# A transformer block on one core: weights loaded behind x, two banks for early V tiles, and a different order of the first head groups

## The chip, the cores and the metric

The kernel runs on one core of a Trainium2 chip. A core has a matrix engine (TensorE, PE in the profile; its weight loads are listed as PEld), a vector engine (VectorE, DVE), a scalar engine (ScalarE, ACT), a general engine (GpSimd, POOL) and a queue engine (SyncE, SP). Each runs its own instructions in order and waits for the others by semaphores. Matrix products are written to PSUM, which has eight banks of 128 partitions by 512 fp32 columns; everything else lies in SBUF. DMAs are issued by an engine's queue, here SP's and, for a few, ACT's.

The metric is the time of one execution on the device, in microseconds. Lower is better.

## The reference

One transformer block with pre-norm, on 2048 rows of 512 features in bf16, with 32 heads of 16:

```python
h  = x + attention(layernorm(x))         # qkv = ln(x) @ wqkv; softmax(q k^T / 4) v; @ wo
h2 = h + glu(layernorm(h))               # (sigmoid(n @ w_gate) * (n @ w_up)) @ w_down, F = 1792
```

Heads are small, so the scores cost little arithmetic in the sums over 16 features; but 32 x 2048 x 2048 exponentials, 134 million, must be taken.

## The kernel before, in words

**Tiling.** Queries are taken in chunks c: three of 512 rows and two of 256. Heads are taken in groups g of four, eight groups in all. For each (c, g), keys are taken in blocks of 128. A *unit* (c, g, k, j) is one head's scores of one block of keys against the query chunk, a 128 x 512 tile, one PSUM bank. Three units make a *step* (`groups`, 683 of them). The main loop runs over the steps, in the order in which `units` lists them.

**A step.** `emit_scores(i)` issues the step's score matmuls (L848) into one of two PSUM tiles of three banks, pss0 and pss1, by turns. ScalarE then takes exp of the 128 x 1536 tile in one instruction (L859). In every fourth step, from step 8 on, one of the three units is taken by VectorE instead, in five instructions (L878 to L891: `exp_bits` and three more), so ScalarE's instruction is 128 x 1024; in `twice` steps a second such unit goes to VectorE in the same four steps. `emit_pv` issues the matmuls of exp with V (L929) some steps later, into the bank `acc`. Each head has V with a column of ones (`Vaug`), which gives the sum for the softmax.

Scores are kept from overflow by a bound per query: the norm of the query times the largest norm of a key, which enters the scores as one more row (`bnd`, `nks`). Query rows of the current head group are spread by DMA over the partitions of `QB` (two buffers, by turns; `emit_q_rows`, `emit_q_bound`), keys over those of `KT` (`k_spread`), both on SP's queue. The odd rows of `KT` hold ones, the unused rows of `QB` zeros; GpSimd's memsets put them there. The first two steps read a QB buffer that has no bound row yet and add the bound by a matmul of their own (L835, L838).

**Pairs.** When `pairs` is true, two heads' score matmuls, of 64 rows each, run side by side in the two halves of the array. It is true in the first 44 steps (`FIRST`), then in odd steps and around `twice` steps, except where the filler is idle.

**Fillers.** All other matrix work is a generator, `filler()`, which yields one matmul at a time: V tiles 3 to 15, then K block 1 and the Q of query chunk 0 for the same heads, blocks 2 and 3 likewise, then Q of query chunks 1 to 3, then each chunk's output projection and feed-forward (`ffn_tasks`). A block is 128 features, eight heads, two head groups. `emit_fill(i)` lets so many matmuls through at each step as `rate(i)` says; `RATES` has the rates by step modulo 4, those of the first 44 steps stand in `rate`. Steps with PV work get fewer. A `("gap", n)` holds the filler back n steps, an `("at", n)` to a step modulo 4, a `("from", n)` to step n. Fillers of this part share one PSUM bank (`ps_misc`), so a tile's matmuls wait until the tile before has been evicted.

**Prologue.** Ahead of the steps, `prologue` loads x, takes the row statistics in eight pairs of 128 rows (`stats` on VectorE, `stats_act` on ScalarE for pair 1, the inverse root on GpSimd), normalises them (`apply`, L317), transposes them on TensorE (`trans`, L324) and copies them to `xnT` on ScalarE (L326). As rows become ready it computes K block 0 in four chunks of 512 (`k_chunk`, `k_half`), Q of chunk 0 for the first eight heads (`q_chunk`), V tiles 0 to 2 (`v_tile`), the key norms, and the bound. It takes its PSUM tiles from a pool of six banks, which is closed before pss0 and pss1 are made of the same banks. The three parts of wqkv are loaded from ScalarE's queue, K's first, beside x on SP's queue.

**The order of the work** is that of the text: each engine runs its instructions in the order in which this program emits them. No scheduler reorders them.

Of the kernel before, what the change touches and what calls it, by code (L numbers as in the profile page):

```python
# [19 lines left out]
def kernel(  # L20
# [28 lines left out]
    RATES = ((2.0, 2.0, 0.0, 3.0), (2.0, 2.5, 0.0, 3.0))  # L49
    FIRST = 44  # L50
    GM = 188
# [19 lines left out]
    def pm_tile():  # L71
        return pmh["pool"].tile([P, 512], FP32, name="pm")
# [154 lines left out]
    qgs = [(c, g) for c in range(NC) for g in range(NG)]  # L227
# [20 lines left out]
    NV0 = 3  # L248
# [4 lines left out]

    def prologue(pro):
# [3 lines left out]
        for part in (1, 0, 2):  # L258
            nc.scalar.dma_start(out=wqkv_sb[:, :, part * D:(part + 1) * D],
                                in_=wqkv_v[:, :, part * D:(part + 1) * D])  # L260
# [3 lines left out]
        nc.gpsimd.memset(QB[1][:].rearrange("p j q -> p (j q)").bitcast(FP32), 0.0)  # L264
# [122 lines left out]
        fill_ones(nc.gpsimd, KT[:, 1, :])  # L387
        stats_act(1)
        nc.gpsimd.memset(QB[0][:].rearrange("p j q -> p (j q)").bitcast(FP32), 0.0)
        nc.gpsimd.memset(bnd[:].bitcast(FP32), 0.0)  # L390
        stats(2)
        nc.gpsimd.memset(Vaug[:, :, :, DH:DH + 1], 1.0)
        apply(0)
        trans(0)
        stats(3)
        apply(1)
        trans(1)
        apply(2)
# [8 lines left out]
        apply(4)  # L407
        k_chunk(1)
        norm_mm_to(acc[:], sqs["q"])
        trans(4)  # L410
        stats(6)
        apply(5)
        v_tile(0)
        norm_part_of(1)
        v_tile(1)
        trans(5)
        stats(7)
        apply(6)
        ps2 = k_mm(2)
        square(2, ps2[:])  # L420
        trans(6)
# [3 lines left out]
        k_max(pnp[0:96, :], km4 := small.tile([P, 1], FP32, name="km4"))  # L425
# [7 lines left out]
        k_copy(2, ps2)  # L433
        k_copy(3, ps3)
# [3 lines left out]
        k_fold(kd, 96, 0)  # L438
        pn3 = ps_misc.tile([P, 512], FP32, name="pm")
# [24 lines left out]
    def first_step(c):  # L464
        return NS * CHUNKS[c][0] / S if c < NC else NS
# [67 lines left out]
    def fill_q(qc):  # L533
# [19 lines left out]
        for b in range(4):  # L553
            ready.add(("b", qc, b))
# [519 lines left out]
```

## Time and profile before

| what | us |
|---|---|
| median of 3 runs | 963.19 |
| the runs | 962.74, 963.19, 966.67 |
| the profiled execution | 966.62 |
| its span, first to last instruction | 964.8 |
| ACT busy | 898.4 (93%) |
| PE busy | 832.2 (86%) |
| DVE busy | 784.4 (81%) |
| POOL busy | 36.0 (4%) |
| first exp of the steps starts at | 35.38 |
| last exp ends at | 934.80 |
| an exp of 128 x 1536 / 128 x 1024 on ACT | 1.473 to 1.486 / 1.058 to 1.068 |

Exps that follow each other without a wait overlap a little, so a row of them takes less than the sum of their lengths. A matmul's end is modelled, so a busy PE isn't PE at its peak. A window of the profile gives, for a stretch of time, the busy time and number of instructions of each engine, the granted share of TensorE's clock, and what the DMA engines moved. Step n starts where the n-th exp activation (L859) starts.

### The profile page before, as it was taken

The numbers are of one execution on the slowest core, as the hardware profiler recorded it, in microseconds if no ns is written. First come the engines' busy times: TensorE is split into PE (matmuls) and PEld (weight loads), VectorE is DVE, ScalarE is ACT, GpSimd is POOL, SyncE is SP. The second block draws the span as 40 slices with busy tenths as digits, with TensorE's granted clock in tenths as the row PEclk, the third lists the DMA queues.
The fourth block names the chain that finished last, engine by engine and source line by source line (L and its number), as shares of the span: only waits on it lengthen the run. The fifth ranks groups of instructions, "written<-read, shape, count | busy, mean of one in ns | idle before, by whom it ended". The sixth has DMA issues, their size and how long they took to land.

```text
span 964.8 us, 17172 instructions
## 1 busy us (share of the span) xinstructions
PE 832.2 (86%) x6335; PEld 338.8 (35%) x6433; DVE 784.4 (81%) x1413; ACT 898.4 (93%) x774; POOL 36.0 (4%) x55
## 2 busy tenths in 40 slices
PE   4888888888888999998788999888788999998998
PEld 2322222222222232222222233222255555555656
DVE  8389998888878888899888888898899788777653
ACT  5789999999999999999999999999998999999872
POOL 5102000000001000000000000000000000000000
PEclk9999999999999999999999999999999999999999
DMA  5102341000013000001011000000011000010010
GB/s 159 24 1 56 113 104 29 16 15 3 15 26 102 15 15 16 9 19 27 15 26 27 16 16 14 4 26 26 16 26 26 16 10 16 27 32 16 9 35 12
DMA packets 37645, 28.45 MB, mean 29 GB/s; under 512 B 17788, under 2 KB 32920, under 8 KB 37560
## 3 DMA queue, kind: packets, MB, share of 16 engines
q1 hardware_dynamic: 35832, 25.64, 10.1%
q10 hardware_dynamic: 1728, 1.70, 0.5%
q8 instruction: 50, 0.82, 0.4%
q14 instruction: 35, 0.29, 0.1%
HBM read 20.31 MB, written 2.61 MB: 24 GB/s over the span
## 4 chain that ended last, share of the span: by engine, by line
PE 43%; DVE 24%; ACT 23%; issue 6%; DMA 2%; SPq 1%; ACTq 0%; DVEq 0%
PE pss L848 20%; ACT pt L859 13%; PE acc L929 8%; PE pm L587 6%; ACT stg L859 4%; ACT wd L859 3%; DVE stg L878 3%; ACT QTu L859 2%; PE pm L603 2%; PE pm L168 2%; DVE reg L881 2%; DVE pt L891 2%; PE pm L163 2%; DVE y L887 2%; PE pm L563 1%
## 5 line engine op out<-in xcount | busy, mean ns | idle before, releaser
L848 PE MATMUL pss<-QB,KT 64*128 64x512 bf16 (+3 forms) x2533 | 475.8, 337 | 81.6 <-ACT pt L859 39.9
L859 ACT ACTIVATE pt<-pss 128x1536 bf16<-128x1536 f32 (+1 forms) x392 | 502.1, 1360 | 17.2 <-PE pss L848 11.5
L848 PEld LDWEIGHTS <-KT 64*128 64x128 bf16 (+1 forms) x2554 | 180.4, 95 | 340.3 <-issue 227.8
L859 ACT ACTIVATE stg<-pss 128x1536 bf16<-128x1536 f32 (+1 forms) x140 | 183.0, 1355 | 4.5 <-PE pss L848 3.8
L878 DVE TENSOR_SCALAR stg<-pss 128x512 int32<-128x512 f32 x123 | 84.8, 689 | 71.6 <-PE pss L848 58.1
L929 PE MATMUL acc<-pt,Vaug 128*17 128x512 bf16 (+1 forms) x1471 | 112.9, 339 | 4.6 <-DVE xs_all L903 3.4
L859 ACT ACTIVATE wd<-pss 128x1536 bf16<-128x1536 f32 (+1 forms) x80 | 103.7, 1387 | 2.5 <-PE pss L848 2.5
L859 ACT ACTIVATE QTu<-pss 128x1024 bf16<-128x1024 f32 (+1 forms) x71 | 95.6, 1346 | 1.7 <-PE pss L848 1.2
L884 DVE SCALAR_TENSOR_TENSOR y<-reg 128x512 f32<-128x512 f32 x123 | 85.2, 692 | 4.2
L887 DVE SCALAR_TENSOR_TENSOR y<-y,reg 128x512 f32<-128x512 f32 x123 | 84.2, 684 | 1.1
L929 PEld LDWEIGHTS <-Vaug 128*17 128x17 bf16 x2560 | 50.5, 89 | 97.5 <-issue 83.0
L587 PE MATMUL pm<-reg,reg 128*128 128x512 bf16 (+1 forms) x252 | 55.6, 333 | 8.8 <-DVE reg L600 6.7
L587 PE MATMUL pm<-reg,wu 128*128 128x512 bf16 (+1 forms) x280 | 58.1, 338 | 1.5 <-ACT sg L592 1.2
L603 PE MATMUL pm<-wd,reg 128*128 128x512 bf16 x173 | 51.2, 381 | 4.9 <-issue 2.9
L881 DVE TENSOR_SCALAR reg<-stg 128x512 int32<-128x512 int32 x123 | 52.0, 423 | 2.0
L929 PE MATMUL acc<-stg,Vaug 128*17 128x256 bf16 (+1 forms) x564 | 51.1, 329 | 0.7 <-DVE stg L891 0.4
L600 DVE SCALAR_TENSOR_TENSOR reg<-sg,pm 128x512 bf16<-128x512 f32 x56 | 38.2, 683 | 14.0 <-PE pm L587 13.5
L891 DVE SCALAR_TENSOR_TENSOR pt<-y,stg 128x512 bf16<-128x512 f32 x70 | 47.7, 682 | 1.8
L592 ACT ACTIVATE sg<-pm 128x512 f32<-128x512 f32 x56 | 35.6, 635 | 10.2 <-PE pm L587 9.9
L878 DVE TENSOR_SCALAR wd<-pss 128x512 int32<-128x512 f32 x45 | 30.9, 688 | 16.8 <-PE pss L848 16.0
L168 PE MATMUL pm<-reg 128*128 128x512 bf16 x114 | 37.0, 403 | 5.7 <-ACT reg L326 3.3
L149 POOL TENSOR_TENSOR rs<-ve,pw_neg 128x1 f32<-128x1 f32 x16 | 11.3, 704 | 813.5 <-DVE ve L147 813.5
(141 smaller groups left out, 712.7 us busy)
## 6 DMA issues: line engine op xcount, KB each, us to landing
rb_all<-rd SPq DMA_DIRECT2D x96, 64.0 KB
xr<-in_A_x_dram SPq DMA_DIRECT2D x16, 128.0 KB
out_dram<-ob SPq DMA_DIRECT2D x15, 128.0 KB
rb_all<-rd SPq DMA_DIRECT2D x60, 32.0 KB
reg<-in_A_x_dram SPq DMA_DIRECT2D x7, 256.0 KB
KT<-stg SPq DMA_DIRECT2D x7, 256.0 KB
reg<-in_B_w_gate_dram SPq DMA_DIRECT2D x4, 448.0 KB
wu<-in_B_w_up_dram SPq DMA_DIRECT2D x4, 448.0 KB
```

Source lines behind the costliest of these rows:

```text
L168: nc.tensor.matmul(ps[:], lhsT=wqkv_sb[:, c, w0:w0 + P], rhs=xnT[:, c, n * QC:(n + 1) * QC], start=(c == 0), stop=(c == DC - 1))
L587: nc.tensor.matmul(ps[:, i * w:(i + 1) * w], lhsT=wt[:, c, f * P:(f + 1) * P], rhs=hnT[:, c, 0:w], start=(c == 0), stop=(c == DC - 1))
L600: nc.vector.scalar_tensor_tensor(out=out, in0=a, scalar=1.0, in1=b, op0=ALU.add, op1=ALU.mult)
L603: nc.tensor.matmul(ps[:], lhsT=hT[:, f, tt * P:(tt + 1) * P], rhs=wd[:, f, :], start=(f == 0), stop=(f == FC - 1))
L848: nc.tensor.matmul(pss[:, ui, h * w:(h + 1) * w], lhsT=KT[rows, g, kt * P:(kt + 1) * P], rhs=QB[n_qg % 2][rows, j, 0:w], start=True, stop= ...
L859: ex = nc.scalar.activation(out=pt[:, 0:na, :], in_=pss[:, 0:na, :], func=ACT.Exp, scale=DH ** -0.5 / QS)
L878: return nc.vector.tensor_scalar(out=e_bits, in0=src, scalar1=ONE_BITS, scalar2=0.0, op0=ALU.add, op1=ALU.max)
L881: nc.vector.tensor_scalar(out=e_man, in0=e_bits, scalar1=0x7FFFFF, scalar2=-0x40800000, op0=ALU.bitwise_and, op1=ALU.bitwise_or)
L884: nc.vector.scalar_tensor_tensor(out=e_pol, in0=m, scalar=PA, in1=m, op0=ALU.add, op1=ALU.mult)
L887: nc.vector.scalar_tensor_tensor(out=e_pol, in0=e_pol, scalar=PB, in1=e_man.bitcast(FP32), op0=ALU.add, op1=ALU.mult)
L891: nc.vector.scalar_tensor_tensor(out=dst, in0=e_pol, scalar=PC, in1=e_bits.bitcast(FP32), op0=ALU.add, op1=ALU.mult)
L929: nc.tensor.matmul(acc[32 * j:32 * j + VW, 0:w], lhsT=Vaug[:, kt, 4 * g + j, :], rhs=p[:, h * w:(h + 1) * w], start=(kt == 0), stop=(kt == ...
```

## The change

It has five parts.

1. The three loads of wqkv move from ScalarE's queue, inside `prologue`, to SP's queue, behind the loads of x.
2. In `prologue`, each pair's transposes come ahead of the K, Q or V tile that stood before them. GpSimd's memsets are cut in halves and put elsewhere (that of the ones in `Vaug` goes to the beginning). The four copies that fill `same` move from VectorE to ScalarE. The copies of K chunks 2 and 3 and V tile 1 come later, V tile 2 is left to the fillers, and `nks` is set at the end. PSUM comes from the six banks of pss0 and pss1 themselves, by turns, instead of a pool of its own.
3. The fillers' V tiles 3 and 5 use the bank `acc`, which is cleared after tile 5.
4. The order of head groups for the first two query chunks becomes (0,0), (0,1), (1,0), (1,1), (0,2) to (0,7), (1,2) to (1,7). K blocks 1 to 3 are thus due 42 steps later, and Q of chunk 1 for the first eight heads is filled ahead of K block 1 (`fill_q1`). What is tied to the end of a chunk (`end_step`: its feed-forward, the `twice` steps) goes by the new order.
5. The rates of fillers become (2, 1, 0, 1) instead of (2, 2, 0, 3) in steps 24 to 511; the rates of the first steps hold until step 24 instead of 44; `GM`, the step at which exp's buffers move to another place, becomes 216.

```diff
-    RATES = ((2.0, 2.0, 0.0, 3.0), (2.0, 2.5, 0.0, 3.0))
+    RATES = ((2.0, 1.0, 0.0, 1.0), (2.0, 2.5, 0.0, 3.0))
     FIRST = 44
-    GM = 188
+    GM = 216
+    VF = 24
...
     def pm_tile():
+        if "banks" in pmh:
+            return next(pmh["banks"])
         return pmh["pool"].tile([P, 512], FP32, name="pm")
...
     for i in range(1, 8):
         nc.sync.dma_start(out=xb[:, 2 * i:2 * i + 2, :], in_=x_v[:, 2 * i:2 * i + 2, :])
+    for part in (1, 0, 2):
+        nc.sync.dma_start(out=wqkv_sb[:, :, part * D:(part + 1) * D],
+                          in_=wqkv_v[:, :, part * D:(part + 1) * D])
...
-    qgs = [(c, g) for c in range(NC) for g in range(NG)]
+    qgs = [(c, g) for g0, g1 in ((0, 2), (2, NG)) for c in range(2) for g in range(g0, g1)]
+    qgs += [(c, g) for c in range(2, NC) for g in range(NG)]
+    at_qg = {qg: n for n, qg in enumerate(qgs)}
...
-    NV0 = 3
+    NV0 = 2
...
-        for part in (1, 0, 2):
-            nc.scalar.dma_start(out=wqkv_sb[:, :, part * D:(part + 1) * D],
-                                in_=wqkv_v[:, :, part * D:(part + 1) * D])
...
-        nc.gpsimd.memset(QB[1][:].rearrange("p j q -> p (j q)").bitcast(FP32), 0.0)
+        clear(QB[1][:])
+        nc.gpsimd.memset(Vaug[:, :, :, DH:DH + 1], 1.0)
...
-            nc.vector.tensor_copy(out=same[r], in_=ident_bf[r, r].unsqueeze(1).to_broadcast([32, 4, H]))
+            nc.scalar.copy(out=same[r], in_=ident_bf[r, r].unsqueeze(1).to_broadcast([32, 4, H]))
...
         apply(2)
+        trans(2)
         k_chunk(0)
-        trans(2)
         stats(4)
         apply(3)
+        trans(3)
+        fill_ones(nc.gpsimd, KT[:, 1, S // 2:S])
         q_chunk()
-        norm_part_of(0)
-        trans(3)
...
-    units = [(c, g, k, j) for c in range(NC) for g in range(NG) for k in range(n_k(c)) for j in range(4)]
+    units = [(c, g, k, j) for c, g in qgs for k in range(n_k(c)) for j in range(4)]
...
-    def first_step(c):
-        return NS * CHUNKS[c][0] / S if c < NC else NS
+    def end_step(c):
+        return (max(n for n, u in enumerate(units) if u[0] == c) + 1) / GU
...
     def fill_v(t):
-        ps = pm_tile()
+        ps = acc if t in (3, 5) else pm_tile()
...
+        if t == 5:
+            nc.vector.memset(acc[:], 0.0)
...
         for t in range(NV0, NT):
             yield from fill_v(t)
+        yield from fill_q1(1, 0)
         for b in range(1, 4):
             yield from fill_k(b)
-            yield from fill_q0(b)
+            yield from fill_q1(0, b)
         for qc in range(1, NQC):
-            yield from fill_q(qc)
+            yield from fill_q(qc, int(qc == 1))
         for c in range(NC - 1):
-            yield ("from", int(first_step(c + 1)) + (11 if c + 3 >= NC else 15))
+            yield ("from", int(end_step(c)) + (11 if c + 3 >= NC else 15))
...
-        if i < FIRST:
+        if i < VF:
             rates = (4.0, 4.0 if i < 6 else 2.0 if i > 16 else 0.0, 4.0 if i < 6 else 0.0, 4.0)
...
-        n0 = int(qc * SPC) + 52
-        for n in range(n0, min(int((qc + 1) * SPC) + 16, int(first_step(NC - 1)) + 14)):
+        n0 = int(end_step(qc - 1)) + 52
+        for n in range(n0, min(int((qc + 1) * SPC) + 16, int(end_step(NC - 2)) + 14)):
...
-        p1ctx = ExitStack()
-        pmh["pool"] = p1ctx.enter_context(tc.tile_pool(name="ps_p1", bufs=6, space=PSUM))
-        prologue(p1ctx.enter_context(tc.tile_pool(name="pro", bufs=1)))
-        p1ctx.close()
-        pmh["pool"] = ps_misc
         sctx = ExitStack()
         ps_s = sctx.enter_context(tc.tile_pool(name="ps_s", bufs=1, space=PSUM))
+        pss2 = [ps_s.tile([P, GU, QC], FP32, name=f"pss{k}") for k in range(2)]
+        pmh["pool"] = ps_misc
+        pmh["banks"] = cycle([t[:, u, :] for t in pss2 for u in range(GU)])
+        with tc.tile_pool(name="pro", bufs=1) as pro:
+            prologue(pro)
+        del pmh["banks"]
```

`fill_q1(qc, b)` is the old `fill_q0(b)` for any query chunk qc. The rest of `prologue` is moved in the same way as the lines shown: `trans(4)`, `trans(5)` and `trans(6)` come ahead of the norm, K or V work that stood before them.

More of the change, by code (lines that the diff above doesn't have):

```diff
@@ L386, in prologue @@
         stats(0)
[L387 removed]
+        clear(QB[0][:, 0:2, :])
         stats_act(1)
[L389 to L390 removed]
         stats(2)
[L392 removed]
         apply(0)
         trans(0)
+        clear(QB[0][:, 2:4, :])
         stats(3)
@@ L445, in prologue @@
                                 scalar2=-SQRT_SLACK, op0=ALU.mult, op1=ALU.mult)
+        nc.vector.tensor_scalar(out=nks[:], in0=z0[:].bitcast(FP32), scalar1=-SQRT_SLACK, scalar2=None, op0=ALU.mult)
         ready.add(("b", 0, 0))
         emit_q_bound(0)
-        v_tile(2)
-        nc.vector.memset(acc[:], 0.0)
         k_spread(ku, 1, slice(0, S), nc.sync)
```

60 lines of the change are left out of this document (33 added, 27 removed).

## The prediction

> **What bounds the kernel now.** I read the windows by stage first, then the timeline of each engine where ACT is not full, then the granted clock. Step n below is the n-th of the 683 exp activations of L859, counted in time order (0 starts at 35.38 us).
>
> The windows view, cut at steps 0, 8, 24, 44 and 56 (columns: stretch, length, busy time and instructions of PE, PEld, DVE, ACT, POOL, granted clock, DMA share, GB/s):
>
> ```profile
> 0.00:35.38 35.38, 18.36 (x113) 9.97 (x116) 24.85 (x72) 18.85 (x32) 14.91 (x30) 1.00 0.37 116
> 35.38:48.03 12.65, 11.51 (x62) 3.61 (x61) 4.07 (x6) 11.29 (x9) 1.84 (x2) 1.00 0.12 26
> 48.03:70.48 22.45, 19.40 (x127) 5.63 (x129) 17.85 (x30) 20.26 (x16) 0.00 (x0) 1.00 0.00 1
> 70.48:98.57 28.09, 23.98 (x148) 6.17 (x149) 25.89 (x50) 25.46 (x21) 5.61 (x4) 0.94 0.18 48
> 98.57:113.50 14.93, 12.99 (x85) 3.88 (x86) 13.44 (x28) 14.93 (x14) 0.00 (x0) 1.00 0.32 85
> 113.50:273.10 159.60, 131.69 (x846) 42.15 (x861) 135.21 (x232) 159.47 (x130) 2.36 (x3) 1.00 0.16 40
> ```
>
> From 98.57 to 273.10 ACT is full: steps 44 to 185 take 174.53/141 = 1.238 us each, the floor wherever exp alone counts. Time off ACT's path is worth nothing there. What can be won lies ahead of 98.57: no exp runs for 35.38 us, then 44 steps take 63.19 us where 1.238 each would be 54.5.
>
> The timeline of DVE, POOL, ACT and PE in the prologue (start, length, engine, line, what; in brackets the idle time before it):
>
> ```profile
> 5.07 0.37 ACTq L259 DMA_DIRECT2D reg<-in_A_wqkv_dram  x1
> 5.49 0.63 ACT L299 ACTIVATE sq<-reg 128x512 bf16<-128x512 bf16 x1 [2.81 <-DMA reg<-in_A_x_dram]
> ...
> 7.99 0.69 DVE L142 BATCH_NORM_STATS2 st<-reg 128x6 f32<-128x512 bf16 x1 [2.42 <-DMA reg<-in_A_x_dram]
> ...
> 12.77 2.27 POOL L392 MEMSET Vaug<- 128x512 bf16 x1
> 12.86 2.64 DVE L317 TENSOR_SCALAR xn<-reg,mvs,rs 128x512 bf16<-128x512 bf16 x2 [0.28 <-POOL rs L284]
> 17.03 0.72 DVE L317 TENSOR_SCALAR xn<-reg,mvs,rs 128x512 bf16<-128x512 bf16 x2
> ...
> 33.75 0.81 PE L835 MATMUL pss<-QB,KT 128*128 128x512 bf16 x3 [0.89 <-ACT Vaug L224]
> ...
> 35.38 4.13 ACT L859 ACTIVATE pt<-pss 128x1536 bf16<-128x1536 f32 x3 [1.89 <-PE pss L838]
> ```
>
> Four delays stand there: the third weight load holds ACT's queue till 5.45, and ACT starts on x at 5.49; tiles 4 and 5 of x reach DVE at 7.99; the normalisation of pair 2 takes 2.64 us beside POOL's memset of Vaug, where its like takes 0.72; and the first scores wait for an eviction.
>
> Steps 2 to 5, on PE and ACT:
>
> ```profile
> 38.15 1.02 PE L163 MATMUL pm<-reg 128*128 128x512 bf16 x4 [0.25 <-DVE Vaug L224]
> 39.11 0.60 PE L848 MATMUL pss<-QB,KT 64*128 64x512 bf16 x3
> 39.96 1.02 PE L163 MATMUL pm<-reg 128*128 128x512 bf16 x4 [0.25 <-DVE Vaug L224]
> ...
> 41.55 1.45 ACT L859 ACTIVATE wd<-pss 128x1536 bf16<-128x1536 f32 x1 [0.35 <-PE pss L848]
> ```
>
> One V tile per step goes through one bank: 1.02 of matmul, then 0.69 of DVE cast, before the next may start. The step is 1.81.
>
> The windows around the granted clock's two dips:
>
> ```profile
> 84.50:87.90 3.40, 1.87 (x13) 0.61 (x10) 3.26 (x5) 3.40 (x4) 3.40 (x2) 1.00 0.23 59
> 87.90:91.30 3.40, 3.40 (x20) 0.52 (x17) 3.30 (x7) 2.82 (x3) 0.09 (x1) 0.51 0.24 56
> 169.90:173.30 3.40, 2.29 (x20) 0.79 (x21) 3.13 (x6) 3.40 (x4) 0.00 (x0) 1.00 0.02 5
> 490.70:494.10 3.40, 1.97 (x10) 0.68 (x8) 3.20 (x6) 3.40 (x4) 0.00 (x0) 1.00 0.24 63
> 494.10:497.50 3.40, 3.40 (x19) 0.57 (x18) 2.24 (x4) 2.55 (x2) 0.00 (x0) 0.50 0.13 40
> ```
>
> Both half-clock stretches of 3.4 us follow one in which PE was busy 55% and 58%; one at 67% was followed by none. Price: steps 36 to 40 took 6.12 us and steps 40 to 44 took 4.90 (1.2); steps 352 to 360 took 11.37 where the eight before took 9.92 (1.45).
>
> **The change, part by part.**
>
> *Prologue, DVE side.* The DMA view shows some 350 GB/s from 3 us until 12 us, x and weights mixed. With x alone ahead, tiles 0 to 5 (0.79 MB; 0.27 MB by 3 us, the rest at 350) are through at 4.5; I take 5.2 (ends: 4.5 and the 7.99 of now). Statistics of pair 2 (1.62) and the apply of pair 0 (0.63) then put its transposes at 7.4 instead of 10.05. The four copies of `same` (1.57 on DVE) go to ACT, between its table load and pair 1, where ACT idles 2.81. Pair 1: landed by 4.3 (my estimate; no weight issue now holds ACT), plus the 4.0 that ACT takes now (5.49 to 9.48), plus 1.0 on POOL: its rs at 9.4, now 10.57. POOL handles pair 2's rs behind it: 10.5, apply done at 11.2, now 15.42. The memset of Vaug now lies beside statistics; the QB memset of now (10.52 to 11.47) lay beside such and they kept 0.69, so I cost it at nothing; if Vaug does hold them, its 2.27 comes back. From there DVE needs the 10.4 it needs now (15.42 to 25.84): last apply done at 21.6, 4.2 earlier.
>
> *Prologue, PE and ACT.* With a pair of transposes ahead of each K, Q or V tile, PE no longer stands behind ACT's copy (three waits of 1.1 at L168). ACT is the next bound. From pair 2's copy (12.3) to the square of K chunk 2 it has five copies at 0.9, seven casts or squares at 0.5 and one V cast at 0.6, in all 8.6, plus about 2 of waits while PE is slow (four matmuls took 1.87 at 14.44, 1.02 at 21.20). Hence 23.4 at its end, now 28.35. SP carries three more issues of 0.5, which may wait for room in the queue (its last x issue waited until 7.98); behind them stands the spread of K chunk 0, needed from 15. The weights themselves come last: 3.67 MB at 350 end near 13, K's third near 10.5, against 12 where it is first used. From the norm of chunk 2 to exp 0 now takes 7.0 (28.39 to 35.38). A V tile (1.0) comes ahead of the last half norm, but step 0's first three matmuls no longer wait for a cast: bnd is done at 34.1 on the old clock, exp 0 at 34.9, so 6.5. Exp 0 at 23.5 + 6.5 = 30: I take **-5.7**. Ends: -2.5 (the 1.95 of the slow apply and the 0.5 at the end alone) and -7.5 (no waits of ACT).
>
> *V through two banks.* Tiles 3 and 5 go to acc. Per step PE then has 0.54 of scores and 0.87 of V, 1.41 against ACT's 1.35; I take 1.45 for 1.81 over four steps: -1.4. Step 2 needs the bound rows, whose DMA is issued 0.7 apart and lands some 1.45 after (a reciprocal's write to its re-read, 81.22 to 82.66); that is 2.2 after bnd, as late as PE wants them: +0.1. Sum **-1.3**, ends 0 and -1.9. One V tile more than now is filled, in steps 21 to 23, where K filled before, at the same rates: 0. The memset of acc (0.48) waits for tile 5's cast; PV, its first user, comes at step 6.
>
> *Half-rate fillers.* Following rate() and the gaps, K block 1 fills steps 31 to 49 instead of 21 to 31, and blocks 2 and 3 end at 79 and 110 instead of 55 and 81; their first uses move from steps 43, 85, 128 to 85, 128, 171. Steps 24 to 44 then have 3 to 4 fill matmuls in four steps, as steps 89 to 172 now (60 in 84), which run at 1.238. So 28.09 becomes 24.75, -3.3, of which 1.2 is the dip. Those steps keep their half-height score pairs (until 44), which use PE little, and the first eight have the fewest fills; I give a dip there an even chance: **-2.7**. Ends: 0 and -3.3.
>
> *Later.* Chunk 0's feed-forward moves from steps 187-320 to 231-364, chunk 1's from 359-492 to 371-504; from 527 on nothing differs. Twenty steps instead of 23 take a second exp on DVE: 3 x (1.473 - 1.059) = 1.2 more for ACT. But the three lay in steps 320 to 352, where steps took 1.243 with them, no less than 1.238; cover gone, it costs 1.2. I take 0. POOL's memsets of KT and the load of wd (later by 28 steps, used at 319) have slack.
>
> **Sum.** -5.7 - 1.3 - 2.7 = -9.7 against the profiled execution of 966.62 (span 964.8): 956.9. The median of the runs shown, 963.19, is 3.4 below it, which I put down mostly to its two dips (2.65). A run without dips loses 1.2 less in the third term than -3.3, so -2.1: 963.2 - 9.1 = 954.1. I say 954.3.
>
> The Trainium skill, "TensorE: Matmul & The Clock Gate", Part 1, says that PE falls to half clock after an idle window of about 3.4 us; by that rule alone no dip would come here, as PE never idles so long, and the third term would be -3.3 in the profiled sum. The two rows at 55% and 58% differ from it, and the measurement decides: a poorly filled window is enough.
>
> **Rivals.**
> (a) *The prologue gives only its lower end*, because ACT, with its copies and `same`, or slow PE sets the pace: -2.5 - 1.3 - 1.6 gives 957.8. For: ACT has 18.85 of work there; against: half of that was waits. Chance 0.15.
> (b) *The clock*, in steps 24 to 185: fewer fillers leave PE under 60% busy in many of the 58 stretches of 3.4 us there, and each dip stalls ACT by 1.2 to 1.45. Seven dips eat the gain; 11 make the kernel slower by 0.5%; 14 give 972. For: both dips fell where fills were few. Against: steps 89 to 172 had no dip at 2.9 fills in four steps, and 131 fills in 162 steps are 3.2, spread more evenly. Chance 0.07.
> (c) *The gain in the prologue isn't there*: the Vaug memset holds the first statistics (2.3), and V's weights, last on the queue, hold PE; with the fillers alone, -2.7, some 961. Chance 0.06.
> (d) *More than forecast*, both first terms at their ends and no dip: -7.5 - 1.9 - 2.1 = -11.5, so 951.7. Chance 0.12.
> The forecast keeps 0.60.
>
> **How the numbers follow.** 954.3 is the likeliest case's; its own range is 952 to 957. Leaving out (b), (c) and a part of (d) and of (a): 949.5 to 959. A half per cent (4.8 us: 958.4 and 968.0) is about what a measurement can tell from none. Faster: the forecast, (d) and most of (a), 0.84; within: (c) and the rest of (a), 0.09; slower: (b), 0.07.
>
> **What would show it.** In the changed profile: exp 0 at 30; the apply of pair 2 at 0.7 and done by 11.2; ACT's first square of x before 5; steps 2 to 5 at 1.45; steps 24 to 44 at 1.24 with at most one dip; steps 44 to 185 still at 1.238; the rest as before. Wrong, if exp 0 comes after 33, or the granted clock shows many dips up to step 185.

## The result, and the profile after

The changed kernel is slower: 974.80 us (median of 4 runs, 973.99 to 975.92) against 963.10 for the kernel before (4 runs, 962.74 to 966.67). The ratio is 1.0114, with a 95% interval of 1.0088 to 1.0140. The forecast was 954.3, so the prediction was wrong, on the other side of no change. The profiled executions are 966.62 (span 964.8) before and 975.92 (span 974.1) after: the 9.3 us to be explained.

The windows view of the kernel after, cut at steps 0, 8, 24, 44 and 185 (stretch, length, busy time and instructions of PE, PEld, DVE, ACT and POOL, granted clock, DMA share, GB/s):

```profile
0.00:46.76 46.76, 25.29 (x109) 12.71 (x112) 23.79 (x68) 19.71 (x36) 14.99 (x32) 1.00 0.28 87
46.76:58.25 11.49, 11.34 (x62) 3.35 (x62) 4.55 (x7) 11.27 (x9) 3.58 (x3) 1.00 0.14 29
58.25:80.70 22.45, 19.40 (x127) 5.64 (x129) 17.88 (x30) 20.25 (x16) 0.00 (x0) 1.00 0.00 1
80.70:105.50 24.80, 21.13 (x138) 6.00 (x138) 21.91 (x39) 24.77 (x21) 0.00 (x0) 1.00 0.12 34
105.50:279.70 174.20, 151.61 (x944) 45.95 (x962) 152.92 (x271) 174.20 (x142) 5.96 (x6) 1.00 0.18 46
```

Only the first stretch grew among these, and by more than the whole kernel did (the lengths by step are from the starts of the exps; the last stretch goes to the last instruction):

| stretch | before, us | after, us | difference | forecast |
|---|---|---|---|---|
| up to exp 0 | 35.38 | 46.76 | +11.38 | -5.7 |
| steps 0 to 8 | 12.65 | 11.49 | -1.16 | -1.3 |
| 8 to 24 | 22.45 | 22.45 | 0.0 | 0 |
| 24 to 44 | 28.09 | 24.80 | -3.29 | -2.7 |
| 44 to 185 | 174.53 | 174.24 | -0.3 | 0 |
| 185 to 527 | 442.0 | 444.7 | +2.7 | 0 |
| 527 to the end | 249.7 | 249.7 | 0.0 | 0 |

Everything from step 0 to step 185 does what the prediction said. The loss is in the prologue. In the 46.76 us PE is busy 25.29 us where it was 18.36 in before, with four matmuls fewer. The timeline of PE in the prologue after (start, length, engine, line, what; in brackets the idle time before it and the releaser) says why in its lengths and in its waits:

```profile
8.52 1.03 PE L333 MATMUL pss<-ident_bf,xn 128*128 128x128 bf16 x8 [8.52 <-POOL nm L311]
11.64 1.03 PE L333 MATMUL pss<-ident_bf,xn 128*128 128x128 bf16 x8 [2.08 <-DVE xn L326]
13.77 1.01 PE L333 MATMUL pss<-ident_bf,xn 128*128 128x128 bf16 x8 [1.10 <-DVE st L148]
14.57 1.91 PE L174 MATMUL pss<-reg 128*128 128x512 bf16 x4
17.72 1.01 PE L333 MATMUL pss<-ident_bf,xn 128*128 128x128 bf16 x8 [1.23 <-DVE xn L326]
19.82 1.87 PE L174 MATMUL pss<-reg 128*128 128x512 bf16 x4 [1.10 <-ACT reg L335]
...
32.78 1.87 PE L174 MATMUL pss<-reg 128*128 128x512 bf16 x4 [1.10 <-ACT reg L335]
```

The timeline of ACT over the same time, and at exp 0:

```profile
4.34 0.63 ACT L308 ACTIVATE sq<-reg 128x512 bf16<-128x512 bf16 x1 [0.56 <-DMA reg<-in_A_x_dram]
...
12.71 1.01 ACT L335 COPY reg<-pss 128x1024 bf16<-128x1024 bf16 x1 [1.76 <-PE pss L333]
14.82 1.01 ACT L335 COPY reg<-pss 128x1024 bf16<-128x1024 bf16 x1 [1.10 <-PE pss L333]
...
18.76 1.01 ACT L335 COPY reg<-pss 128x1024 bf16<-128x1024 bf16 x1 [1.10 <-PE pss L333]
...
46.76 5.57 ACT L873 ACTIVATE pt<-pss 128x1536 bf16<-128x1536 f32 x4 [1.94 <-PE pss L852]
```

Read the two together. The transposes of pair 2 (PE, 13.77) begin when ACT's copy of pair 1 ends (12.71 + 1.01 = 13.72). They go into another bank than that copy reads, and they read nothing that it writes. The bank is the next third of the same tile, pss0. The profile puts the wait down to DVE's statistics at L148, which end at 13.76, just as the transposes start; but the transposes don't read them, and the rows of `xn` that they do read were done at 13.16. In the same way Q's matmuls (19.82) begin when the copy of pair 3 ends (19.77), whose bank lies in the same tile pss1. And ACT waits in its turn: it stands idle for 1.10 while the transposes run that its next copy reads. PE and ACT take turns. In all, PE stands seven times behind an ACT read of another bank of the same tile, at 13.77, 19.82, 23.77, 26.85, 32.78, 38.36 and 42.33, for 0.67 to 1.22 each and 7.1 us together.

DVE is drawn into it late in the prologue. It waits for a matmul of PE's, and the normalisation of the last pair stands behind that:

```profile
28.33 0.68 DVE L202 TENSOR_SCALAR y<-acc 32x512 int32<-32x512 int32 x1 [4.03 <-PE acc L374]
28.94 0.71 DVE L326 TENSOR_SCALAR xn<-reg,mvs,rs 128x512 bf16<-128x512 bf16 x2
```

The second thing is the length. Four matmuls of 512 columns still take 1.87 at 32.78. In before they took 1.87 early on and 1.02 from 21.20 on:

```profile
14.44 1.87 PE L168 MATMUL pm<-reg 128*128 128x512 bf16 x4 [1.10 <-ACT reg L326]
21.20 1.02 PE L168 MATMUL pm<-reg 128*128 128x512 bf16 x4 [1.10 <-ACT reg L326]
```

So 1.87 is their length at half clock. The clock column reads 1.00 throughout, because the trace has no record of the clock before its first change; here the lengths tell the clock. In before the trace first grants the full clock at 19.7, after at 45.7. The windows of 3.4 us that end at these times, and windows before them, in before:

```profile
12.90:16.30 3.40, 2.30 (x11) 1.04 (x9) 3.37 (x5) 1.01 (x1) 3.08 (x3) 1.00 0.02 6
16.30:19.70 3.40, 3.40 (x18) 1.58 (x16) 3.29 (x11) 2.79 (x5) 1.28 (x3) 1.00 0.08 19
```

and after:

```profile
28.70:32.10 3.40, 2.85 (x13) 1.20 (x11) 0.95 (x3) 1.18 (x3) 0.00 (x0) 1.00 0.07 17
32.40:35.80 3.40, 2.27 (x5) 0.51 (x4) 0.00 (x0) 0.93 (x2) 0.00 (x0) 1.00 0.00 0
35.50:38.90 3.40, 2.14 (x12) 1.27 (x12) 1.17 (x3) 0.58 (x1) 0.00 (x0) 1.00 0.02 5
42.30:45.70 3.40, 3.14 (x7) 1.01 (x7) 1.15 (x5) 1.05 (x2) 0.00 (x0) 1.00 0.16 39
```

Windows in which PE is busy 63%, 67% or even 84% change nothing; after one of 100% (before) or 92% (after) the full clock is there. The Trainium skill, "TensorE: Matmul & The Clock Gate", Part 1, says that PE's default is the half clock and that it goes to full after a busy window of about 3.4 us. These rows agree. So waits that spread PE's work thinly may cost twice: by their own length, and by keeping PE at half clock.

### The profile page after: what moved, and what is told of

The parts are those of the page before. It is cut to its first block, busy times and chain, and to the rows that moved or that the text cites. A ratio compares the mean times of both kernels' runs of the same rounds, so it can differ in the third digit from the quotient of the medians.

```text
span 974.1 us, 17161 instructions
## 1 busy us (share of the span) xinstructions
PE 842.5 (86%) x6335; PEld 340.2 (35%) x6433; DVE 777.4 (80%) x1398; ACT 899.6 (92%) x777; POOL 35.8 (4%) x57
## 4 chain that ended last, share of the span: by engine, by line
PE 44%; ACT 24%; DVE 23%; issue 6%; DMA 2%; SPq 0%; POOL 0%; ACTq 0%; DVEq 0%
PE pss L862 21%; ACT pt L873 13%; PE acc L943 8%; PE pm L600 6%; ACT stg L873 4%; ACT wd L873 4%; DVE stg L892 3%; PE pm L616 2%; ACT QTu L873 2%; DVE pt L905 2%; PE pm L576 2%; DVE reg L895 2%; DVE y L901 2%; DVE reg L613 1%; DVE y L898 1%
## 5 line engine op out<-in xcount | busy, mean ns | idle before, releaser
L873 ACT ACTIVATE stg<-pss 128x1536 bf16<-128x1536 f32 (+1 forms) x132 | 172.7, 1359 | 5.0 <-PE pss L862 3.2
L892 DVE TENSOR_SCALAR stg<-pss 128x512 int32<-128x512 f32 x116 | 80.0, 690 | 73.3 <-PE pss L862 62.1
L873 ACT ACTIVATE wd<-pss 128x1536 bf16<-128x1536 f32 (+1 forms) x92 | 119.3, 1391 | 0.8 <-PE pss L862 0.5
L873 ACT ACTIVATE QTu<-pss 128x1024 bf16<-128x1024 f32 (+1 forms) x67 | 91.0, 1358 | 2.2 <-PE pss L862 1.5
L898 DVE SCALAR_TENSOR_TENSOR y<-reg 128x512 f32<-128x512 f32 x116 | 80.3, 692 | 4.0
L901 DVE SCALAR_TENSOR_TENSOR y<-y,reg 128x512 f32<-128x512 f32 x116 | 79.5, 685 | 1.0
L892 DVE TENSOR_SCALAR wd<-pss 128x512 int32<-128x512 f32 x52 | 35.9, 690 | 25.0 <-PE pss L862 23.6
L895 DVE TENSOR_SCALAR reg<-stg 128x512 int32<-128x512 int32 x116 | 49.1, 424 | 2.0
L943 PE MATMUL acc<-stg,Vaug 128*17 128x256 bf16 (+1 forms) x540 | 48.0, 324 | 1.4 <-DVE stg L905 0.9
L898 DVE SCALAR_TENSOR_TENSOR wd<-reg 128x512 f32<-128x512 f32 x52 | 36.0, 693 | 1.8
```

The costliest lines, as they stand in the source:

```text
L873: ex = nc.scalar.activation(out=pt[:, 0:na, :], in_=pss[:, 0:na, :], func=ACT.Exp, scale=DH ** -0.5 / QS)
L892: return nc.vector.tensor_scalar(out=e_bits, in0=src, scalar1=ONE_BITS, scalar2=0.0, op0=ALU.add, op1=ALU.max)
L895: nc.vector.tensor_scalar(out=e_man, in0=e_bits, scalar1=0x7FFFFF, scalar2=-0x40800000, op0=ALU.bitwise_and, op1=ALU.bitwise_or)
L898: nc.vector.scalar_tensor_tensor(out=e_pol, in0=m, scalar=PA, in1=m, op0=ALU.add, op1=ALU.mult)
L901: nc.vector.scalar_tensor_tensor(out=e_pol, in0=e_pol, scalar=PB, in1=e_man.bitcast(FP32), op0=ALU.add, op1=ALU.mult)
L943: nc.tensor.matmul(acc[32 * j:32 * j + VW, 0:w], lhsT=Vaug[:, kt, 4 * g + j, :], rhs=p[:, h * w:(h + 1) * w], start=(kt == 0), stop=(kt == ...
```

## The experiments

Theory 1 is that reading: the prologue's PSUM tiles became slices of two tiles of three banks, a tile is guarded as a whole, and so a write to one bank waits for a read of another. 1a says that the clock it keeps down is a large part of the cost, 1b that the serial waits alone are. Theory 2 is that the new order of transposes, loads and copies is itself slower and leaves PE too thinly filled. Theory 3 is that GpSimd's memset of half of KT, which waited 3.79 us for the spread of K chunk 0 and has the inverse roots behind it on POOL, holds the prologue. Exp 0 is the first exp of the steps, as before. Ratios are to the kernel before, on the same chip.

### Own banks for the prologue (e1_own_banks)

The kernel after, with the pool of six single banks of the kernel before:

```diff
-        pmh["banks"] = cycle([t[:, u, :] for t in pss2 for u in range(GU)])
-        with tc.tile_pool(name="pro", bufs=1) as pro:
-            prologue(pro)
-        del pmh["banks"]
+        p1ctx = ExitStack()
+        pmh["pool"] = p1ctx.enter_context(tc.tile_pool(name="ps_p1", bufs=6, space=PSUM))
+        prologue(p1ctx.enter_context(tc.tile_pool(name="pro", bufs=1)))
+        p1ctx.close()
+        pmh["pool"] = ps_misc
```

> The changed kernel with one part undone: the prologue draws its PSUM tiles from a pool of six one-bank tiles of its own again, instead of the six banks of pss0 and pss1. Theory 1 (tracking): PE waits for ACT's read of another bank of the same three-bank tile, which spreads PE's work out and keeps its clock at half. It expects no waits of 1.1 of the transposes for ACT's copy, full clock before 22 us, exp 0 at 29 to 34 instead of 46.8, total 958 to 963. Theory 2 (order): the pair of transposes ahead of each K, Q or V tile waits for VectorE's apply and so leaves PE too sparse to reach full clock, whatever the banks. It expects exp 0 above 42, total above 970. Theory 3 (memset): GpSimd's memset of the second half of KT's group 1 waits 3.8 for the spread of K chunk 0 and holds pair 5's rs. It expects exp 0 unchanged within 1 us.

Measured: 959.74, ratio 0.9952 (0.9936 to 0.9969). Exp 0 is at 31.77, 15.0 earlier than after and 3.6 earlier than before. The timeline of PE:

```profile
12.82 1.03 PE L333 MATMUL pm<-ident_bf,xn 128*128 128x128 bf16 x8 [0.23 <-DVE xn L326]
13.69 1.87 PE L174 MATMUL pm<-reg 128*128 128x512 bf16 x4
15.35 1.06 PE L333 MATMUL pm<-ident_bf,xn 128*128 128x128 bf16 x8
16.20 1.71 PE L174 MATMUL pm<-reg 128*128 128x512 bf16 x4
17.75 0.61 PE L333 MATMUL pm<-ident_bf,xn 128*128 128x128 bf16 x8
```

and its windows:

```profile
14.20:17.60 3.40, 3.40 (x16) 1.70 (x15) 3.29 (x11) 2.64 (x4) 1.03 (x2) 1.00 0.00 0
0.00:31.77 31.77, 17.30 (x111) 9.57 (x112) 23.67 (x68) 19.14 (x36) 14.92 (x32) 1.00 0.41 129
```

PE's seven waits for reads of other banks are gone, PE is full from 14.2 to 17.6, and at 17.6 the full clock comes: the eight transposes of 17.75 take 0.61 where those of 15.35 took 1.06. One edit turns slower by 1.1% into faster by 0.5%. Exp 0 comes 3.6 earlier than in the kernel before, so the new order of the prologue is a gain, and theory 2 falls.

### GpSimd's memset of KT ahead of its wait (e2_memset_early)

The kernel after:

```diff
-        fill_ones(nc.gpsimd, KT[:, 1, 0:S // 2])
+        fill_ones(nc.gpsimd, KT[:, 1, :])
         apply(2)
...
-        fill_ones(nc.gpsimd, KT[:, 1, S // 2:S])
         q_chunk()
```

> The changed kernel with GpSimd's memset of KT's group 1 in one piece ahead of K chunk 0, so that it can't wait for that chunk's spread. Theory 3 expects DVE's wait of 2.04 for rs at 21.31 to go, and exp 0 at 34 to 43. Theory 1 expects PE to keep its waits for ACT's copies and its half clock: exp 0 at 44.5 to 47, total 972 to 975. Theory 2 expects the same as theory 1.

Measured: 973.1, ratio 1.0089 (1.0072 to 1.0107); exp 0 at 45.84, 0.9 earlier than after. The memset's wait is real and small beside 11.4: theory 3 is not the cause. The clock wavered here: full from 31.6 to 35.0, half to 45.2, then full.

### The kernel before with shared banks (e3_before_shared_banks)

```diff
     def pm_tile():
+        if "banks" in pmh:
+            return next(pmh["banks"])
...
-        pmh["pool"] = p1ctx.enter_context(tc.tile_pool(name="ps_p1", bufs=6, space=PSUM))
+        pmh["banks"] = cycle([t[:, u, :] for t in pss2 for u in range(GU)])
```

> The kernel before with one part of the change alone: its prologue draws its PSUM tiles from the banks of pss0 and pss1. Theory 1 expects waits of transposes and K matmuls for ACT's copies, the clock at half beyond 30 us, exp 0 at 42 to 47 instead of 35.4, total 970 to 975. Theories 2 and 3 expect exp 0 at 34 to 36 (the wait for the pool's end gone) and 961 to 964.

Measured: 978.29, ratio 1.0143 (1.0120 to 1.0165); exp 0 at 50.59 where the kernel before has 35.38. This one part of the change costs the kernel before 15.2 us at exp 0, as much as taking it out gave in e1. The size was underestimated (42 to 47 and 970 to 975 were expected): the full clock comes only at 50.6, so that the whole prologue runs at half clock. The timeline of PE shows the lengths and the waits:

```profile
18.05 1.87 PE L170 MATMUL pss<-reg 128*128 128x512 bf16 x4 [1.29 <-ACT reg L328]
...
28.40 1.87 PE L165 MATMUL pss<-reg 128*128 128x512 bf16 x4 [1.10 <-ACT reg L328]
```

### The new steps with the old prologue (e4_old_prologue)

The kernel after, but `prologue`, its pool, its loads and NV0 = 3 as in the kernel before; what is left of the change is parts 3 to 5:

```diff
-    NV0 = 2
+    NV0 = 3
...
-            nc.scalar.copy(out=same[r], in_=ident_bf[r, r].unsqueeze(1).to_broadcast([32, 4, H]))
+            nc.vector.tensor_copy(out=same[r], in_=ident_bf[r, r].unsqueeze(1).to_broadcast([32, 4, H]))
...
+        for part in (1, 0, 2):
+            nc.scalar.dma_start(out=wqkv_sb[:, :, part * D:(part + 1) * D],
+                                in_=wqkv_v[:, :, part * D:(part + 1) * D])
...
```

> The changed kernel with the whole prologue, its pool and the weight loads of the kernel before, and the changed steps. All theories put the loss in the prologue and expect exp 0 at 35.4, steps 0 to 44 in 58.7 (as in the changed kernel) instead of 63.2, steps 185 to 527 2 to 3 slower than before, total 960 to 962.5. A rival that puts a part of the loss in the steps expects 965 or more.

Measured: 967.19 (9 runs), ratio 1.0035 (1.0023 to 1.0046). That is outside the 960 to 962.5 expected and where the rival, a part of the loss in the steps, had put it. Exp 0 is at 34.84, steps 0 to 8 take 11.73 and steps 24 to 44 take 24.67, as expected. But steps 44 to 185 take 177.72 where all others take 174.2 to 175.9. One step, at 172, carries it. PE in the timeline:

```profile
172.14 0.38 PE L861 MATMUL pss<-QB,KT 128*128 128x512 bf16 x1 [2.37 <-DMA QB<-bnd]
```

SP's queue at that place:

```profile
165.90 1.20 SPq L221 DMA_DIRECT2D KT<-stg  x2
167.20 3.21 SPq L240 DMA_DIRECT2D QB<-QTu  x4
170.46 1.27 SPq L250 DMA_DIRECT2D QB<-bnd  x2
```

and SP's queue at the same place in the run with own banks:

```profile
156.56 2.46 SPq L243 DMA_DIRECT2D QB<-QTu  x4
159.07 1.25 SPq L253 DMA_DIRECT2D QB<-bnd  x2
...
167.02 1.83 SPq L224 DMA_DIRECT2D KT<-stg  x2
```

With one V tile fewer for the fillers, the spread of K block 3 comes a little ahead of the next head group's Q rows in SP's queue instead of behind them. SP waits 5.8 us at the spread, until 165.9, for the last of the four casts of the K block on DVE, which ends at 165.83, and the Q rows and the bound wait behind it. Scores then wait 2.37 us, and a half-clock stretch follows (172.6 to 176). So this run doesn't price the fillers well, and it shows how near the new filler order is to such a stall. The kernel after itself hasn't got it: its steps 44 to 185 take 174.24, so this stall is no part of its loss.

### PE kept busy with idle matmuls (e8_warm_pe)

The kernel after, its shared banks kept, with matmuls of no use into `acc` put between the prologue's own: 12 before the first transposes, 8 behind them, 3 or 4 at nine later places.

```diff
+        def warm_pe(n):
+            for _ in range(n):
+                nc.tensor.matmul(acc[:], lhsT=ident_bf[:], rhs=xb[:, 0, :], start=True, stop=True)
...
+        warm_pe(12)
         trans(0)
+        warm_pe(8)
```

> The changed kernel, banks left as they are, with idle matmuls (x tile 0 against the identity, into acc) put where PE waits in the prologue: 12 ahead of the first transposes, 3 to 8 at ten later places. They add work alone; what they raise is PE's clock. Theory 1a (the half clock is most of the loss, and the waits for the other banks only bring it about): full clock before 15 us and held, a K chunk's four matmuls at 1.02 instead of 1.87 and eight transposes at 0.61 instead of 1.03 all through, exp 0 at 34 to 38 instead of 46.8. Theory 1b (the serial waits themselves are most of it): the clock rises too, but exp 0 stays above 42. If the clock doesn't rise, the run says nothing on either.

Measured: 968.32, ratio 1.0038 (1.0022 to 1.0053); exp 0 at 38.76, the full clock from 7.3 on. The timeline of PE:

```profile
3.53 4.58 PE L292 MATMUL acc<-reg,ident_bf 128*128 128x512 bf16 x12 [3.53 <-DMA reg<-in_A_x_dram]
...
13.82 1.03 PE L174 MATMUL pss<-reg 128*128 128x512 bf16 x4
...
17.78 1.02 PE L174 MATMUL pss<-reg 128*128 128x512 bf16 x4 [0.24 <-ACT reg L340]
...
20.88 1.02 PE L174 MATMUL pss<-reg 128*128 128x512 bf16 x4 [1.31 <-ACT reg L340]
```

The lengths are those of the full clock, and waits on ACT's copies are still there. This splits the 15.0 us between after (46.76) and own banks (31.77): 8.0 go with the clock (46.76 - 38.76), and 7.0 with the serial waits (38.76 - 31.77), the idle matmuls' own time included. The split is a rough one. A slower PE also makes the waits longer, and that counts here as clock (ACT's waits for a pair's transposes are 1.10 in after and 0.69 here); own banks runs at half clock until 17.6 and this kernel only until 7.3, so the waits alone may cost somewhat more than 7.0. That PE does more work and exp 0 still comes 8.0 earlier than in after can't come from the waits alone. So 1b falls. Of 1a the clock's part holds, but 38.76 lies above the 34 to 38 that it gave: the clock is about half of the loss, not most of it.

### Own banks and the memset of KT early (e5_banks_memset)

The edits of e1 and e2 together.

> Own banks for the prologue, as in the run before, and GpSimd's memset of KT's group 1 in one piece ahead of K chunk 0. There GpSimd waited 2.96 for the spread at 18.85, and DVE 1.20 for rs at 20.39. Theory 3, in what is left of it, expects exp 0 at 30.3 to 31.2 instead of 31.8 and 958 to 959.5. If ACT or PE sets the pace there, exp 0 stays within 0.4 of 31.8.

Measured: 959.66, ratio 0.9949 (0.9934 to 0.9964). Exp 0 at 30.45, 1.3 earlier than with own banks alone, but the medians are the same. In the profiled run a clock dip at 258.9 makes steps 44 to 185 take 175.61 instead of 174.35; all four runs here have a granted clock of 0.998, as the profiled one has, where four of the five with own banks have 1.000.

### Vaug's memset behind the statistics (e6_banks_both_memsets)

e5, and GpSimd's memset of the ones in Vaug taken from the beginning to behind the last statistics:

```diff
-        nc.gpsimd.memset(Vaug[:, :, :, DH:DH + 1], 1.0)
         nc.vector.memset(ones_blk[:], 0.0)
...
         stats(7)
+        nc.gpsimd.memset(Vaug[:, :, :, DH:DH + 1], 1.0)
         apply(6)
```

> The same, with the memset of Vaug's ones put behind the last pair's root instead of at the beginning, where the copies to ones_blk took 3.45 and the first statistics 1.87 instead of 0.69 beside it. If that memset holds DVE, the first statistics start at 3.3 and take 0.69, the apply of pair 0 moves from 8.1 to 7.0 or less, and exp 0 comes 0.5 to 1.5 earlier than with the KT memset alone. If pair 1's path over ACT sets the pace of what follows (rs of pair 1 at 11.0), exp 0 moves by less than 0.3.

Measured: 958.9, ratio 0.9941 (0.9924 to 0.9957); exp 0 at 30.30. What the memset touches shows on DVE. The kernel after, with the memset from 3.06 to 5.32 on GpSimd:

```profile
1.95 3.45 DVE L282 COPY ones_blk<-head_of 128x32 bf16<-128x32 bf16 x4
3.52 1.87 DVE L148 BATCH_NORM_STATS2 st<-reg 128x6 f32<-128x512 bf16 x1
```

and this run:

```profile
1.95 1.25 DVE L281 COPY ones_blk<-head_of 128x32 bf16<-128x32 bf16 x4
3.44 0.69 DVE L148 BATCH_NORM_STATS2 st<-reg 128x6 f32<-128x512 bf16 x1 [0.23 <-DMA reg<-in_A_x_dram]
...
21.82 2.64 DVE L325 TENSOR_SCALAR xn<-reg,mvs,rs 128x512 bf16<-128x512 bf16 x2
```

At the beginning the memset held DVE's copies until it ended, and the statistics behind them. Taken away from there, it holds the normalisation of pair 7 for the same 2.64 that pair 2 paid in the kernel before. The cost moves with it, and the start gains little, as DVE then waits 1.54 for the next tiles of x (until 6.68) and the normalisation of pair 0 is at 8.30, not at the 7.0 expected. At exp 0, 0.15 is left of the gain. The other memsets do the same where they meet a normalisation: in the run with the loads alone, further down, that of pair 1 took 1.58 (from 10.58 on) beside the memset of QB (10.49 to 11.44), and 0.73 in the kernel before. The Trainium skill, "SBUF — State Buffer", section "SBUF: two separate sides", says that GpSimd and a VectorE instruction in a two-port mode exclude each other for a whole instruction; the 2.64 agrees with it, and no run here tells this lock from another mechanism.

### One `twice` step less (e7_no_322)

In after, steps 185 to 527 are 2.7 slower. `twice` takes every 16th step up to n0 + 56 and every 12th behind it, and with the new n0 this turn puts 322 and 326 into neighbouring groups of four. e6, with:

```diff
+    twice.discard(322)
     split |= twice
```

> The same, with step 322 taken out of the steps in which a second exp goes to VectorE. In the run with own banks steps 326 to 333 took 10.46 (1.494 each), where the steps around took 1.19 to 1.25; 322 and 326 lie in neighbouring groups of four. If VectorE is overrun by two such groups in a row, steps 319 to 340 take 26.0 to 26.6 instead of 27.34 and the total is 0.8 to 1.5 less than without this edit. If ACT is the bound there, it is 0.4 more.

Measured: 956.34, ratio 0.9918 (0.9903 to 0.9933). The window of steps 319 to 340 in e6:

```profile
439.74:467.09 27.35, 23.45 (x150) 6.58 (x148) 24.46 (x42) 25.55 (x22) 0.00 (x0) 1.00 0.07 20
```

and in this run:

```profile
437.90:463.46 25.56, 23.47 (x150) 7.27 (x148) 21.66 (x37) 25.54 (x23) 0.00 (x0) 1.00 0.07 21
```

DVE has 2.8 us less work there and the stretch is 1.8 shorter, with ACT's work the same: two second exps in neighbouring groups were more than DVE could take in time. That is more than the 0.7 to 1.3 expected, and the median fell by 2.6; two of e6's four runs have a granted clock of 0.998, of these four only one.

### Vaug's memset in quarters (e9_vaug_quarters)

e7, with the memset cut in four, each behind the statistics of one of pairs 3 to 6:

```diff
         stats(3)
+        nc.gpsimd.memset(Vaug[:, 0:4, :, DH:DH + 1], 1.0)
...
         stats(4)
+        nc.gpsimd.memset(Vaug[:, 4:8, :, DH:DH + 1], 1.0)
...
         stats(7)
-        nc.gpsimd.memset(Vaug[:, :, :, DH:DH + 1], 1.0)
```

> The last version (own banks, KT memset early, no 322), with the memset of Vaug's ones in four pieces, one behind each of the statistics of pairs 3 to 6, where VectorE is in statistics and not in copies. As one piece it took 2.26 and drew the copies beside it (at the beginning: to ones_blk, 3.45; at the end: apply of pair 7, 2.64 instead of 0.72) out to its own end. If statistics are not held by it, each piece of about 0.57 costs nothing, the last apply ends 1.9 earlier, and exp 0 comes at 28.0 to 28.8 instead of 29.8 to 30.3, total 954.5 to 956. If ACT or PE sets the pace at the end of the prologue, exp 0 stays above 29.3.

Measured: 955.48, ratio 0.9906 (0.9890 to 0.9921), the lowest of all (its interval overlaps that of e7) and faster than both kernels. Exp 0 is at 29.36, no dip in the profiled run. GpSimd's quarter in the timeline:

```profile
12.27 0.64 POOL L402 MEMSET Vaug<- 128x128 bf16 x1
```

and DVE beside it, and at pair 7:

```profile
12.48 0.66 DVE L148 BATCH_NORM_STATS2 st<-reg 128x6 f32<-128x512 bf16 x1
...
21.57 0.74 DVE L325 TENSOR_SCALAR xn<-reg,mvs,rs 128x512 bf16<-128x512 bf16 x2
```

The statistics beside a quarter keep their length, and pair 7 is back at 0.74. The gain at exp 0 is small: e7, whose prologue is that of e6, had exp 0 at 29.79 and e6 at 30.30, so that single runs differ by 0.5 there, and the 0.4 between e7 and e9 is not shown. DVE's last normalisation ends 1.6 earlier than in e7 (22.31 for 23.94) and exp 0 doesn't follow; above 29.3 was the sign given for ACT or PE setting the pace there.

### The loads alone (e10_loads_alone)

The kernel before, with only its weights' loads moved behind x on SP's queue:

```diff
+    for part in (1, 0, 2):
+        nc.sync.dma_start(out=wqkv_sb[:, :, part * D:(part + 1) * D],
+                          in_=wqkv_v[:, :, part * D:(part + 1) * D])
...
-        for part in (1, 0, 2):
-            nc.scalar.dma_start(out=wqkv_sb[:, :, part * D:(part + 1) * D],
-                                in_=wqkv_v[:, :, part * D:(part + 1) * D])
```

> The kernel before with one part of the change alone: the loads of wqkv behind x on SP's queue. The prediction's step expects the statistics of pair 2 at 6.4 instead of 7.99, ACT's first work on x at 4.4 instead of 5.49, and the first transposes at 8.5 instead of 10.05; the apply of pair 2 still meets the memset of Vaug. If that memset sets what follows, exp 0 comes at 34.5 to 35.5, total within 1 of before; if not, at 33 to 34.4.

Measured: 965.38 (10 runs), ratio 1.0014 (0.9999 to 1.0030); exp 0 at 34.37. Two rows of the timeline of DVE tell how little of an earlier x is left:

```profile
6.08 0.69 DVE L145 BATCH_NORM_STATS2 st<-reg 128x6 f32<-128x512 bf16 x1 [0.52 <-DMA reg<-in_A_x_dram]
...
12.83 2.64 DVE L317 TENSOR_SCALAR xn<-reg,mvs,rs 128x512 bf16<-128x512 bf16 x2 [0.67 <-POOL rs L284]
```

Tiles 4 and 5 are there 1.9 earlier (7.99 in before), and the normalisation of pair 2 starts where it did (12.86), since it still meets Vaug's memset. The load order by itself is worth 1.0 at exp 0 and nothing in the time. 34.37 lies just inside the range that was given for the memset not setting what follows; the row of pair 2 says that it does.

### Fillers at full rate (e11_full_rate) and one bank for V (e12_one_bank)

e9 with the rates of the kernel before:

```diff
-    RATES = ((2.0, 1.0, 0.0, 1.0), (2.0, 2.5, 0.0, 3.0))
+    RATES = ((2.0, 2.0, 0.0, 3.0), (2.0, 2.5, 0.0, 3.0))
...
-    VF = 24
+    VF = 44
```

> The first kernel of this batch with the filler rates of before: (2, 2, 0, 3), and the first steps' rates until 44. K block 1 is then filled in steps 29 to 39 instead of 31 to 49. Theory: late due steps are no gain by themselves, the half rate is; it expects steps 24 to 44 at 26 to 28 instead of 24.8, total 1.2 to 3 more. Rival: 28.09 of the kernel before came from its dip and from K block 1's own chain; then steps 24 to 44 take 25.4 or less and the total is the same within 0.7.

e9 with all of the fillers' V tiles in the one bank:

```diff
-        ps = acc if t in (3, 5) else pm_tile()
+        ps = pm_tile()
```

> The first kernel of this batch with V tiles 3 and 5 in the fillers' one bank as before. The prediction's step expects steps 0 to 8 at 12.6 to 12.9 instead of 11.43 and everything else unchanged, total 1.2 to 1.5 more. If not the bank but the DMA of the bound rows held step 2, the difference is below 0.7.

Measured: e11 959.16, ratio 0.9946 (0.9927 to 0.9965), steps 24 to 44 in 27.54 where e9 has 24.81. e12 956.91, ratio 0.9924 (0.9906 to 0.9942), steps 0 to 8 in 12.65 where e9 has 11.43. So the half rate is worth 2.7 us in its stretch and the second bank 1.2, each in the place where the prediction had it. In the whole time the half rate is worth 3.7, more than the 1.2 to 3 expected; 0.7 of it lies in steps 44 to 185 (175.01 for 174.35).

## Why the prediction was wrong

The step that failed is in "Prologue, PE and ACT": "With a pair of transposes ahead of each K, Q or V tile, PE no longer stands behind ACT's copy (three waits of 1.1 at L168)". The order of the instructions allows that. But the change also moves the prologue's PSUM from six tiles of one bank to slices of two tiles of three banks, and the prediction gave that no cost and no bound. The slices made PE stand behind ACT: instead of three such waits gone there were seven, 7.1 us together, each for a read of a bank that the waiting matmul didn't touch. With PE spread thin no window before 42.3 was full enough, and the clock stayed at half until 45.7. Own banks (31.77) against after (46.76) measure it at 15.0, about half of it the clock. The term was -5.7 and came out as +11.38, that is -3.6 for the order and +15.0 for the banks.

By the other steps:

- *DVE side.* The last normalisation was to be done at 21.6, 4.2 earlier than before, and was done at 29.65 (28.94 + 0.71), 3.8 later, behind the wait of 4.03 for PE. With own banks it was done at 24.72 and in e9 at 22.31, so the sum itself was near. ACT began on x at 4.34 (forecast: before 5). Two things on the way were not as forecast. Pair 2 was done at 13.16, not 11.2. And Vaug's memset, costed "at nothing" because statistics lie beside it, held the copies of `ones_blk` (3.45 instead of 1.25), which lie there too, and the first statistics behind them (1.87 instead of 0.69). What the row of the QB memset had shown of statistics is true (0.66 beside a quarter in e9); what it didn't cover were the copies.
- *From the last normalisation to exp 0* the forecast had 8.4 us (30 - 21.6), and before took 9.5 (35.38 - 25.84). It took 17.1 after (46.76 - 29.65), 7.1 with own banks and 7.1 in e9. So 7.6 of the 11.4 lie here and 3.8 ahead of it; both go when the banks are apart.
- *The sum for the prologue.* 12.3 + 8.6 + 2 is 22.9, where the prediction went on with 23.4, and an exp 0 at 30 is 5.4 earlier than 35.38, not 5.7. Neither slip matters beside 15.0.
- *The size of the order's gain.* -5.7 was forecast; own banks give -3.6, with the memset of KT out of the way -4.9 (30.45), and e9 -6.0 (29.36). POOL's memset of KT, which waited for a DMA with the inverse roots behind it, was not in the prediction: "POOL's memsets of KT ... have slack" was said of the later ones.
- *V through two banks.* -1.3 forecast, -1.16 measured, 1.22 in e12. Right.
- *Half-rate fillers.* -2.7 was forecast, which is -3.3 with an even chance of a dip; no dip came and it was -3.29. 24.75 us was given for the stretch without a dip and 24.80 measured. Right.
- *Later.* 0 forecast, +2.7 measured in steps 185 to 527. 1.2 of it lie in steps 319 to 340 (27.35 for 26.11), with the two neighbouring `twice` steps that e7 parted (25.55 there). The prediction missed them: it counted how many `twice` steps there are (three fewer) and not how far apart they lie. Both profiled runs have one dip in this stretch, at 335.8 and 494.1; the rest isn't taken apart.
- *The rivals.* (a) named a slow PE in the prologue, but only as a smaller gain. (b) named the clock, but in steps 24 to 185, where no dip came. (c) had a prologue without its gain, by Vaug's memset, which is worth 1.1 at most (30.45 in e5, 29.36 in e9). No rival had PSUM in it. Of the two signs given for a wrong prediction the first, exp 0 after 33, is the one that came.
- *The clock rule.* That a poorly filled window suffices for half clock held: the windows of 3.4 us ahead of the dips at 335.8 in after and at 258.9 in e5 are filled 57% and 58%. It cuts both ways: the poorly filled prologue of after didn't get the full clock until 45.7. The prediction used "four matmuls took 1.87 at 14.44, 1.02 at 21.20" as a given, and didn't ask what had raised the clock in between (the full window 16.3 to 19.7) and whether the change kept it.

With the banks alone put apart, the change gives 959.74 against 964.53 of the kernel before on the same chip: 4.8 faster, where 9.1 was forecast. So the part of the diff that was left out of the sum decides the direction, and the rest still falls short: the prologue gains 3.6 instead of 5.7, and steps 185 to 527 lose 1.4 (443.4 for 442.0). Only with two memsets moved and one `twice` step taken out as well, which the change didn't have, does it come to 955.48 against 964.27, 8.8 faster; that this is near 9.1 is not a success of the forecast.

The Trainium skill, "PSUM — Partial Sum Buffer", section "PSUM bank collisions raise a hardware error", gives as its rule to guard PSUM by bank and quadrant, not by address. Own banks are guarded by bank and give 31.77; a guard over three banks gives 46.76. That is a cost of how the tiles are declared, and the runs show no limit of the chip in it.

## What to carry to other kernels

When a change moves buffers, ask what the smallest unit is that the program guards: here a slice of a larger tile waited for users of the whole tile, and the releaser that the profile names may be one whose result the waiting instruction doesn't read. When a change thins out an engine's work near the start, look for the window that raises PE's clock and see whether it survives; half clock nearly doubles the matmuls until then, as in 1.87 for 1.02 here. Price every line of a diff, above all those that look like bookkeeping: the one line with `cycle` cost 15.0 us at exp 0, more than the others together gained.

## What the runs showed of the hardware that was not expected

PE at half clock does not need to be idle to stay there: over 46 us of the prologue it was busy 54% (25.29 of 46.76), windows of 3.4 us at 63%, 67% and 84% busy left the clock as it was, and windows at 92% and 100% raised it. Twelve matmuls of no use ahead of the first transposes bring the full clock at 7.3, and with work of no use in between it stayed. Even with the useless work added, that kernel was 6.5 us faster than the same one without (968.32 for 974.80, in different sets of runs; 1.0038 for 1.0114 against the kernel before).

GpSimd's memset of one bf16 in every block of Vaug took 2.26 us for 128 x 512 elements and 0.64 for a quarter. It stretched VectorE's copies and normalisations (1.25 to 3.45, 0.74 to 2.64) and left the statistics beside a quarter as they were (0.66).
